# One VectorE pass fewer in turning float64 weights into float32

## The chip, the cores and the metric

The kernel runs on one core of a Trainium2 chip. The metric is the device time of one execution in microseconds, given as the median of a few runs; the less, the better.

## The reference

Three parts follow one another. First an attention over 16 heads (2 x 8) of 768 positions with 64 columns each, in which a query sees only keys of the same hash bucket; then two MLPs without bias, each 512 to 2048 to 512, over 1536 tokens.

```python
q_bits = (np.einsum('bhsd,dk->bhsk', q, proj) > 0)      # k_bits alike, six bits each
mask = q_bucket[:, :, :, None] == k_bucket[:, :, None, :]
scores = np.where(mask, scale * np.matmul(q, k.transpose(0, 1, 3, 2)), -1e9)
...
x = attn_out.transpose(0, 2, 1, 3).reshape(1536, 512)
h = x @ w_in;  x = (h / (1 + np.exp(-1.702 * h))) @ w_out       # first MLP
h = x @ w_in2; x = (h / (1 + np.exp(-h))) @ w_out2              # second MLP
```

`q`, `k`, `v` are float32, but the four weight matrices arrive as float64: they were scaled by a float64 number when drawn. No engine here works in float64, so the kernel takes each weight as two 32-bit words and builds the float32 value out of their bits.

## The kernel before, in words

**Weights.** Both MLPs cut their 2048 hidden columns into 16 blocks of 128. A block has two chunks, one of `w_in` and one of `w_out`, of 128 x 512 values each. There are 64 chunks in all. A chunk is loaded as int64 into `raw` (two buffers; L165 in the first MLP, L229 in the second), and `convert` (L113) makes float32 of it in `f`: ScalarE reads the upper word as if it were a float (L121), and four VectorE passes clamp it, shift its exponent, put the sign back and add the three lowest bits from the lower word (L122, L123, L124, L126). The value under work is `u`, one buffer in PSUM; for the first four chunks, which are converted before that buffer exists, it is `f` itself, in SBUF. Then `halves` (L130) splits `f` into a rounded half and the rest: ScalarE copies (L131), GpSimd subtracts (L132). The names `wih`, `wil`, `woh`, `wol` are these halves. In the first MLP 13 of the 16 blocks are also written to DRAM (L196, `spih` and so on) and read back later (L188).

**Attention.** Each of 96 steps takes 128 queries of a head: scores on TensorE (L520, L521) into `pss`, the row's minimum on VectorE (L528) into `p`, the exponential on ScalarE (L533), its f16 halves (L542 or L544, and L548 on GpSimd) in `hl`, a DMA that transposes two steps at once into `pt` (L554, on the queue of SP), and the product with `v` (L566 to L568) into `pav`. The result is turned and split into `XH` and `XL` (L594 to L601).

**Weaving.** After half of the heads the first batch is ready, and the first MLP works on it while attention goes on with the second batch: L742 is its first product, L721 to L726 its gate, L762 its second product, L771 the sum. Later the first MLP takes the second batch, and the second MLP (L807, L864, L874) ends the kernel. The second MLP forms some weights as sums of blocks (L283 to L286).

**What sets the order.** The code only says what depends on what. A planner places the instructions on the queue of each engine by priorities (the table `SOONER`, L80) and by its own simulated clock, and each engine then works its queue in order. A change in what one pass is thought to take can therefore move work on all engines.

Of the kernel before, what the change touches and what calls it, by code (L numbers as in the profile page):

```python
# [9 lines left out]
F32 = mybir.dt.float32  # L10
# [4 lines left out]
AF = mybir.ActivationFunctionType  # L15
ALU = mybir.AluOpType
# [5 lines left out]
def tile_lsh_attention_two_mlps(  # L22
# [13 lines left out]
    V, A, G, T, SP = nc.vector, nc.scalar, nc.gpsimd, nc.tensor, nc.sync  # L36
# [18 lines left out]
    VTOP = 2.0 ** 14  # L55
    MASK = 2.0 ** 30

    TINY = 2.0 ** -15
    HUGE = 122880.0 - 2.0 ** -7
    QSCALE = -1.0 / math.sqrt(D)  # L60
    assert math.frexp(QSCALE)[0] == -0.5
    NBUF = 3
# [50 lines left out]
    def convert(raw):  # L113
        word = raw.bitcast(I32).rearrange("p c (e w) -> p c e w", w=2)
        f = wpool.tile([P, NDC, P], F32, tag="f", name="f", bufs=FB)
        fi = f.bitcast(I32)

        u = work[0].tile([P, NDC, P], F32, tag="u", name="u") if work[0] is not None else f
        ui = u.bitcast(I32)
        top, bot = word[:, :, :, 1], word[:, :, :, 0]  # L120
        A.activation(u, top.bitcast(F32), AF.Abs)  # L121
        V.tensor_scalar(u, u, TINY, HUGE, op0=ALU.max, op1=ALU.min)  # L122
        V.tensor_scalar(ui, ui, 3, 0x3FFFFFFF, op0=ALU.logical_shift_left, op1=ALU.bitwise_and)  # L123
        V.scalar_tensor_tensor(out=ui, in0=top, scalar=-0x40000000, in1=ui,  # L124
                               op0=ALU.bitwise_and, op1=ALU.bitwise_or)
        V.scalar_tensor_tensor(out=fi, in0=bot, scalar=29, in1=ui,  # L126
                               op0=ALU.logical_shift_right, op1=ALU.bitwise_or)
        return f
# [5 lines left out]
    class Weights:  # L134
# [40 lines left out]
        def step(self):  # L175
            n = self.done
            while self.issued <= min(n + 1, len(self.chunks) - 1):
                self.fetch()
            i, kind = self.chunks[n]
            pool = self.pool_of(i)[0]  # L180
            hi = pool.tile([P, NDC, P], F32R, tag=f"w{kind}h", name=f"w{kind}h")
            lo = pool.tile([P, NDC, P], F32R, tag=f"w{kind}l", name=f"w{kind}l")
            block = self.order[i]
            self.t[i, kind] = hi, lo
            self.done += 1
            if self.again(n):
                for t, d in zip((hi, lo), self.kept.pop((block, kind))):
                    SP.dma_start(out=t.bitcast(F32), in_=d)  # L188
                return
            f = convert(self.raw.pop(n))  # L190
            halves(hi, lo, f)
            if self.last[block] > i:
                self.kept[block, kind] = []
                for t, part in ((hi, "h"), (lo, "l")):
                    d = spill.tile([P, NDC, P], F32, name=f"sp{kind}{part}{block[1]}")
                    SP.dma_start(out=d, in_=t.bitcast(F32))  # L196
                    self.kept[block, kind].append(d)
# [8 lines left out]
    class Pairs:  # L206
# [42 lines left out]
        def step(self):  # L249
# [4 lines left out]
            if how == "back":  # L254
                f = wpool.tile(whole, F32, tag="f", name="f", bufs=FB)
                SP.dma_start(out=f, in_=self.kept.pop(key))
            else:
                while len(self.raw) < 2 and self.sources:
                    self.fetch()
                f = convert(self.raw.pop(key))  # L260
# [846 lines left out]
```

## Time and profile before

| | |
|---|---|
| median of 3 runs | 789.61 us (784.69 to 790.25) |
| the profiled execution | 786.58 us |
| its span, first to last instruction | 784.8 us |
| mean granted TensorE clock | 0.972 of full speed |
| busy share PE / DVE / ACT / POOL | 92% / 71% / 56% / 62% |
| bytes moved by DMA | 124.82 MB, 159 GB/s over the span |

PE is TensorE, DVE VectorE, ACT ScalarE, POOL GpSimd; SP is the engine that only issues DMAs. A busy share is an average over a program with several regimes, so the rows below are cut by stretches: attention alone up to about 136 us, attention woven with the first MLP up to about 395 us, and the MLPs alone from there. A wait names the engine that was idle and the instruction that ended its idle time. The chain of waits follows the last instruction back to what released it, step by step; its shares say where the span went. DMA's share is the mean busy share of the 16 DMA engines and can pass 1, since packets overlap.

### The profile page before, as it was taken

What the parts mean: (1) busy time and instruction counts of PE and PEld (TensorE: products, weight loads), DVE (VectorE), ACT (ScalarE), POOL (GpSimd) and SP (SyncE); (2) the same over time, 40 slices, a digit from 0 to 9 for tenths busy, and PEclk for the clock granted to TensorE, in tenths of its full rate; (3) what the DMA queues carried; (4) which work ended last, traced back from release to release, by engine and by line L of the source; (5) the groups of instructions that cost most, each with busy time, mean ns of one, the idle gap of its engine ahead of it and who ended that gap; (6) DMA issues with size and microseconds to landing.
All of it is one profiled execution on the core that took longest, in us unless ns stands there. A gap on an engine that the chain in (4) does not pass through costs nothing.

```text
span 784.8 us, 14279 instructions
## 1 busy us (share of the span) xinstructions
PE 722.9 (92%) x5288; PEld 663.8 (85%) x5288; DVE 553.6 (71%) x1028; ACT 441.0 (56%) x767; POOL 488.1 (62%) x423
## 2 busy tenths in 40 slices
PE   6786777779899899899989999999999999999998
PEld 5676666668788899899989999999999998899886
DVE  8977688976789888797545777768334454687554
ACT  5866575777868677667556334445535333445330
POOL 5676576867667767567799624649627727457431
PEclk9898889799999999999999999999999999999999
DMA  5998999999998999797697675640001102021004
GB/s 161 188 202 192 185 195 211 214 248 225 270 254 244 255 255 265 192 222 174 106 320 255 230 257 175 212 136 0 28 1 55 55 0 54 28 81 53 1 2 160
DMA packets 200883, 124.82 MB, mean 159 GB/s; under 512 B 153831, under 2 KB 176359, under 8 KB 200813
## 3 DMA queue, kind: packets, MB, share of 16 engines
q1 hardware_dynamic: 200652, 123.91, 63.2%
q8 instruction: 41, 0.67, 0.3%
q14 instruction: 30, 0.24, 0.1%
q10 hardware_dynamic: 160, 0.00, 0.0%
HBM read 60.82 MB, written 20.97 MB: 104 GB/s over the span
## 4 chain that ended last, share of the span: by engine, by line
PE 65%; DMA 16%; DVE 7%; ACT 4%; issue 4%; POOL 3%; SPq 1%; DVEq 0%; POOLq 0%
PE psh L864 17%; PE psp L807 15%; DMA pt<-hl 11%; PE psp L762 6%; PE psp L742 6%; PE psh L742 5%; PE pso L762 5%; PE psh L762 3%; POOL hl L548 3%; DVE p L528 2%; PE pss L520 2%; ACT p L533 2%; DMA raw<-in_moe_w_out_dram 2%; PE pss L521 1%; PE pav L566 1%
## 5 line engine op out<-in xcount | busy, mean ns | idle before, releaser
L726 POOL TENSOR_TENSOR gl<-g,gh 128x384 fp32r<-128x384 f32 x128 | 129.2, 1017 | 130.2 <-ACT gh L725 117.3
L548 POOL TENSOR_TENSOR hl<-p,hl 128x768 f16<-128x768 f32 x96 | 162.7, 1702 | 71.3 <-ACT hl L544 34.6
L533 ACT ACTIVATE p<-p,lo 128x768 f32<-128x768 f32 x96 | 89.6, 937 | 51.8 <-DVE p L528 51.4
L874 DVE TENSOR_TENSOR part<-psh,part 128x512 f32<-128x512 f32 x84 | 58.1, 691 | 67.6 <-PE psh L864 67.3
L528 DVE TENSOR_SCALAR_CACHE_REDUCE p<-pss 128x768 f32<-128x768 f32 x96 | 90.8, 948 | 14.9 <-PE pss L521 13.2
L725 ACT CAST gh<-g 128x384 fp32r<-128x384 f32 x128 | 64.2, 512 | 52.5 <-PE psh L864 42.2
L566 PE MATMUL pav<-VS,pt 128*128 128x65 f16 x576 | 66.2, 200 | 29.4 <-DMA pt<-hl 27.5
L566 PEld LDWEIGHTS <-pt 128*128 128x128 f16 x576 | 55.6, 101 | 39.6 <-DMA pt<-hl 34.5
L520 PE MATMUL pss<-ak,aq 128*128 128x384 f32 x192 | 75.0, 392 | 10.3 <-DVE p L528 10.1
L724 ACT ACTIVATE g<-psp 128x384 f32<-128x384 f32 x88 | 43.2, 491 | 64.1 <-POOL gl L726 29.4
L864 PE MATMUL psh<-wol,gh 128*128 128x512 f32 x192 | 75.8, 395 | 0.0
L864 PE MATMUL psh<-woh,gl 128*128 128x512 f32 x192 | 75.6, 394 | 0.0
L864 PE MATMUL psh<-woh,gh 128*128 128x512 f32 x192 | 74.6, 389 | 0.0
L122 DVE TENSOR_SCALAR u<-u 128x512 f32<-128x512 f32 x60 | 41.7, 695 | 41.0 <-ACT u L121 40.9
L521 PE MATMUL pss<-BK,BQ 128*128 128x384 f32 x192 | 68.0, 355 | 0.0
L567 PE MATMUL pav<-VS,pt 128*128 128x64 f16 x576 | 66.3, 201 | 0.0
L568 PE MATMUL pav<-VS,pt 128*128 128x65 f16 x576 | 65.9, 199 | 0.0
L544 ACT CAST hl<-p 128x768 f16<-128x768 f32 x77 | 63.6, 829 | 2.1 <-DMA pt<-hl 1.1
L121 ACT ACTIVATE u<-raw 128x512 f32<-128x512 f32 x60 | 38.1, 634 | 45.1 <-DMA raw<-in_moe_w_out_dram 15.4
L132 POOL TENSOR_TENSOR wol<-f,woh 128x512 fp32r<-128x512 f32 x32 | 41.1, 1295 | 32.9 <-PE psh L864 20.4
L567 PEld LDWEIGHTS <-pt 128*128 128x128 f16 x576 | 56.4, 102 | 3.2 <-issue 3.2
L568 PEld LDWEIGHTS <-pt 128*128 128x128 f16 x576 | 56.5, 103 | 1.1 <-issue 1.1
(210 smaller groups left out, 2230.7 us busy)
## 6 DMA issues: line engine op xcount, KB each, us to landing
raw<-in_moe_w_in_dram SPq DMA_DIRECT2D x32, 512.0 KB
raw<-in_moe_w_out_dram SPq DMA_DIRECT2D x32, 512.0 KB
spih<-wih SPq DMA_DIRECT2D x13, 256.0 KB
spil<-wil SPq DMA_DIRECT2D x13, 256.0 KB
spoh<-woh SPq DMA_DIRECT2D x13, 256.0 KB
spol<-wol SPq DMA_DIRECT2D x13, 256.0 KB
wih<-spih SPq DMA_DIRECT2D x13, 256.0 KB
wil<-spil SPq DMA_DIRECT2D x13, 256.0 KB
```

The lines of the kernel that those rows point to most:

```text
L520: T.matmul(o, lhsT=lq, rhs=ak[:, half, :], start=True, stop=False)
L528: V.tensor_scalar(p, st.pop(("S", j)), LOW, None, op0=ALU.min, op1=ALU.min, accum_out=lo)
L533: A.activation(p, p, AF.Exp, bias=lo, scale=-1.0)
L548: G.tensor_tensor(out=hl[:, 1], in0=st.pop(("p", j))[0], in1=hl[:, 0], op=ALU.subtract)
L566: T.matmul(o, lhsT=pt[:, i], rhs=hv, start=(i == 0), stop=False)
L567: T.matmul(o[:, 0:D], lhsT=pt[:, i], rhs=lv, start=False, stop=False)
L568: T.matmul(o, lhsT=pt[:, NC + i], rhs=hv, start=False, stop=(i == NC - 1))
L726: G.tensor_tensor(out=gl, in0=g, in1=gh.bitcast(F32), op=ALU.subtract)
L742: T.matmul(h, lhsT=a[:, c], rhs=x[:, c, span(t)], start=(n == 0), stop=(n == 3 * NDC - 1))
L762: T.matmul(y, lhsT=w[:, o], rhs=g[:, f], start=(n == 0), stop=(n == 3 * nf - 1))
L807: T.matmul(o, lhsT=a, rhs=b, start=(n == 0), stop=(n == 5))
L864: T.matmul(y, lhsT=a[:, f, os_], rhs=x, start=(n == 0), stop=(n == 5))
```

## The change

ScalarE no longer takes the absolute value of the upper word but multiplies it by 2 to the power of -112, which lowers the exponent field in place. The clamp (L122) goes with its two constants. The next pass shifts left by three and masks nothing, since the shift itself drops the sign. The sign is then taken from the upper word by one bit in place of two.

```diff
--- before.py
+++ after.py
@@ -55,8 +55,7 @@
     VTOP = 2.0 ** 14
     MASK = 2.0 ** 30
 
-    TINY = 2.0 ** -15
-    HUGE = 122880.0 - 2.0 ** -7
+    DOWN = 2.0 ** -112
     QSCALE = -1.0 / math.sqrt(D)
     assert math.frexp(QSCALE)[0] == -0.5
     NBUF = 3
@@ -118,10 +117,9 @@
         u = work[0].tile([P, NDC, P], F32, tag="u", name="u") if work[0] is not None else f
         ui = u.bitcast(I32)
         top, bot = word[:, :, :, 1], word[:, :, :, 0]
-        A.activation(u, top.bitcast(F32), AF.Abs)
-        V.tensor_scalar(u, u, TINY, HUGE, op0=ALU.max, op1=ALU.min)
-        V.tensor_scalar(ui, ui, 3, 0x3FFFFFFF, op0=ALU.logical_shift_left, op1=ALU.bitwise_and)
-        V.scalar_tensor_tensor(out=ui, in0=top, scalar=-0x40000000, in1=ui,
+        A.activation(u, top.bitcast(F32), AF.Copy, scale=DOWN)
+        V.tensor_scalar(ui, ui, 3, None, op0=ALU.logical_shift_left)
+        V.scalar_tensor_tensor(out=ui, in0=top, scalar=-0x80000000, in1=ui,
                                op0=ALU.bitwise_and, op1=ALU.bitwise_or)
         V.scalar_tensor_tensor(out=fi, in0=bot, scalar=29, in1=ui,
                                op0=ALU.logical_shift_right, op1=ALU.bitwise_or)
```

Lines of the changed kernel stand two lower from the old L123 on and one lower before: the old L123 is L121, L124 is L122, L126 is L124, L165 is L163, L196 is L194, L520 is L518, L528 is L526, L554 is L552, L594 is L592 and L762 is L760.

The planner also places the work anew from the first conversion on. Three places show how.

VectorE, the first two conversions, which come before the first MLP's first product (`f` and `raw` as above; L528 makes `p`, L601 `XL`, L408 a rounded copy of `q` or `k`), before:

```order
L122 TENSOR_SCALAR f<-f 128x512
L528 TENSOR_SCALAR p,lo<-pss 128x768
L123 TENSOR_SCALAR f<-f 128x512
L601 TENSOR_TENSOR XL<-psx,XH 128x384
L408 CAST sq<-nq 128x6x64
L124 SCALAR_TENSOR_TENSOR f<-raw,f 128x512
L528 TENSOR_SCALAR p,lo<-pss 128x768
L601 TENSOR_TENSOR XL<-psx,XH 128x384
L122 TENSOR_SCALAR f<-f 128x512
L126 SCALAR_TENSOR_TENSOR f<-raw,f 128x512
L578 TENSOR_SCALAR ri<-pav,sv 128x3
L542 CAST hl<-p 128x768
```

and now:

```order
L121 TENSOR_SCALAR f<-f 128x512
L526 TENSOR_SCALAR p,lo<-pss 128x768
L122 SCALAR_TENSOR_TENSOR f<-raw,f 128x512
L599 TENSOR_TENSOR XL<-psx,XH 128x384
L406 CAST sq<-nq 128x6x64
L526 TENSOR_SCALAR p,lo<-pss 128x768
L124 SCALAR_TENSOR_TENSOR f<-raw,f 128x512
L599 TENSOR_TENSOR XL<-psx,XH 128x384
L121 TENSOR_SCALAR f<-f 128x512
L540 CAST hl<-p 128x768
```

The four passes of a conversion are three, and the passes between them are the same ones in nearly the same order; the second conversion begins one row after the first has ended, where it began one row before.

SP, the DMAs around the 24th and 25th transpose (`raw` a load of weights, `sp..` halves written to DRAM, L432 and L384 loads for attention), before:

```order
L165 DMA raw<-in_moe_w_out_dram 128x512
L196 DMA spih_2208<-wih 128x512
L554 DMA_TRANSPOSE pt<-hl 128x24x128
L196 DMA spil_2210<-wil 128x512
L165 DMA raw<-in_moe_w_in_dram 128x4x128
L554 DMA_TRANSPOSE pt<-hl 128x24x128
L196 DMA spoh_2315<-woh 128x512
L196 DMA spol_2317<-wol 128x512
L165 DMA raw<-in_moe_w_out_dram 128x512
L554 DMA_TRANSPOSE pt<-hl 128x24x128
```

and now:

```order
L163 DMA raw<-in_moe_w_out_dram 128x512
L194 DMA spih_2205<-wih 128x512
L552 DMA_TRANSPOSE pt<-hl 128x24x128
L194 DMA spil_2207<-wil 128x512
L163 DMA raw<-in_moe_w_in_dram 128x4x128
L194 DMA spoh_2311<-woh 128x512
L163 DMA raw<-in_moe_w_out_dram 128x512
L552 DMA_TRANSPOSE pt<-hl 128x24x128
L194 DMA spol_2313<-wol 128x512
L552 DMA_TRANSPOSE pt<-hl 128x24x128
```

A load of `raw` that stood behind the second transpose in these rows stands ahead of it.

TensorE, where the first MLP's second product begins (`pso` its sums; `pss` scores, `psx` the turn of a finished block, `pstr` of a new head, `pav` the product with `v`), before:

```order
L416 MATMUL pstr<-identr,sq 128x128 x3
L520 MATMUL pss<-ak,aq 128x384
L521 MATMUL pss<-BK_153,BQ_149 128x384
L520 MATMUL pss<-ak,aq 128x384
L521 MATMUL pss<-BK_153,BQ_149 128x384
L594 MATMUL psx<-ident,xn 128x128 x3
L762 MATMUL pso<-gh,woh 128x384 x2
L416 MATMUL pstr<-identr,sq 128x128 x3
L566 LDWEIGHTS pt
```

and now:

```order
L519 MATMUL pss<-BK_152,BQ_148 128x384
L760 MATMUL pso<-gh,woh 128x384 x2
L518 MATMUL pss<-ak,aq 128x384
L519 MATMUL pss<-BK_152,BQ_148 128x384
L518 MATMUL pss<-ak,aq 128x384
L519 MATMUL pss<-BK_152,BQ_148 128x384
L760 MATMUL pso<-gl,woh 128x384
L760 MATMUL pso<-gh,wol 128x384
L760 MATMUL pso<-gh,woh 128x384
L760 MATMUL pso<-gl,woh 128x384
L760 MATMUL pso<-gh,wol 128x384
L760 MATMUL pso<-gh,woh 128x384
```

Before, two products of L762 stood ahead of the weight load of `pt` that ends the first piece and begins the `pav` of a pair. Now 18 of them stand ahead of that same weight load, 16 more.

## Rows read from the trace of the kernel before

**Rows 1.** Page, part 1: busy us, share of the span, instructions of each engine.

```profile
PE 722.9 (92%) x5288; PEld 663.8 (85%) x5288; DVE 553.6 (71%) x1028; ACT 441.0 (56%) x767; POOL 488.1 (62%) x423
```

**Rows 2.** Windows view, five stretches: length, busy us (instructions) of each engine, clock, DMA.

```profile
core 0: us, PE busy (x) PEld busy (x) DVE busy (x) ACT busy (x) POOL busy (x), PEclk, DMA share, GB/s
0.00:136.00 136.00, 101.56 (x1068) 85.65 (x1069) 110.65 (x236) 91.09 (x134) 89.10 (x68) 0.89 0.92 189
136.00:172.00 36.00, 25.87 (x298) 22.51 (x296) 31.01 (x57) 23.91 (x37) 24.89 (x16) 0.86 1.07 234
172.00:280.00 108.00, 99.34 (x896) 90.49 (x897) 85.00 (x165) 81.48 (x138) 78.42 (x62) 0.98 1.07 251
280.00:395.00 115.00, 112.45 (x1014) 107.00 (x1014) 90.79 (x185) 79.44 (x130) 79.94 (x62) 1.00 0.84 195
395.00:785.00 390.00, 383.69 (x2019) 358.14 (x2017) 236.10 (x389) 165.04 (x333) 215.77 (x217) 1.00 0.32 105
```

**Rows 3.** Chain of waits in 395 to 785 us, shares by line.

```profile
by line: PE psh L864 34.0%; PE psp L807 30.0%; PE psp L762 12.1%; PE psp L742 11.7%; PE psh L762 5.1%; PE psh L742 4.3%; DMA wih<-spih 1.0%; ACT L724 0.3%; DVE part L874 0.2%; ACT u L121 0.2%; ACT gh L725 0.1%; ACT g L724 0.1%; SPq L188 0.1
```

**Rows 4.** Waits of PE, 136 to 172, then 172 to 280: us, times, longest.

```profile
PE pav L566 <- DMA pt<-hl: 3.2, 2, 2.7
PE pss L520 <- DVE p L528: 3.1, 4, 1.8
PE psh L742 <- DVE XL L601: 1.6, 1, 1.6
...
PE pav L566 <- DMA pt<-hl: 5.7, 5, 1.5
```

**Rows 5.** Groups by line and form: count, busy us, mean ns, idle before.

```profile
L122 DVE TENSOR_SCALAR u<-u 128x512 f32<-128x512 f32 x60 | 41.7, 695 | 41.0 <-ACT u L121 40.9
L122 DVE TENSOR_SCALAR f<-f 128x512 f32<-128x512 f32 x4 | 2.7, 671 | 2.4 <-ACT f L121 2.4
L123 DVE TENSOR_SCALAR u<-u 128x512 int32<-128x512 int32 x60 | 41.7, 694 | 0.9
L121 ACT ACTIVATE u<-raw 128x512 f32<-128x512 f32 x60 | 38.1, 634 | 45.1 <-DMA raw<-in_moe_w_out_dram 15.4 <-DMA raw<-in_moe_w_in_dram 14.6 <-DVE f L126 13.9
L423 ACT ACTIVATE aq<-pstr 128x384 fp32r<-128x384 f32 x32 | 15.4, 488 | 6.0 <-PE pstr L416 5.8
L528 DVE TENSOR_SCALAR_CACHE_REDUCE p<-pss 128x768 f32<-128x768 f32 x96 | 90.8, 948 | 14.9 <-PE pss L521 13.2 <-POOL hl L548 1.5
```

**Rows 6.** Source view: L121 on `f`; L122 in 172:280, 280:395, 395:785 (min/median/max ns).

```profile
L121 ACT ACTIVATE f<-raw x4: 661/674/719, 137.0 to 164.8; 128x512 f32<-128x512 f32 x4
...
L122 DVE TENSOR_SCALAR u<-u x15: 677/695/700, 181.6 to 276.3; 128x512 f32<-128x512 f32 x15
...
L122 DVE TENSOR_SCALAR u<-u x13: 680/696/700, 283.9 to 361.7; 128x512 f32<-128x512 f32 x13
...
L122 DVE TENSOR_SCALAR u<-u x32: 689/699/700, 395.1 to 724.3; 128x512 f32<-128x512 f32 x32
```

**Rows 7.** Chain of waits in order of time: L122 in 136 to 280 (start, us).

```profile
165.46 0.04 DVE f L122
...
190.49 0.70 DVE u L122
...
221.38 0.71 DVE u L122
...
240.32 0.61 DVE u L122
...
246.98 0.68 DVE u L122
```

**Rows 8.** Chain of waits by line, 172 to 280, then 280 to 395.

```profile
by line: DMA pt<-hl 26.1%; issue 8.9%; DMA nv<-in_v_dram 6.9%; POOL hl L548 5.9%; DMA raw<-in_moe_w_in_dram 5.1%; DVE p L528 4.9%; PE pso L762 4.5%; DMA raw<-in_moe_w_out_dram 3.5%; ACT p L533 2.9%; DVE u L122 2.5%; PE pav L566 2.3%; POOL g
...
by line: PE pso L762 27.5%; PE psh L742 20.2%; DMA pt<-hl 17.3%; PE pss L520 5.0%; PE pss L521 4.6%; PE pav L566 3.7%; PE pav L567 3.3%; PE pav L568 3.2%; DMA raw<-in_moe_w_out_dram 3.1%; PE psbit L448 2.4%; SPq L188 1.4%; POOL hl L548 1.4%
```

**Rows 9.** Page, part 6, size of a load; chain of waits, 24 products back to back.

```profile
raw<-in_moe_w_in_dram SPq DMA_DIRECT2D x32, 512.0 KB
...
285.86 4.16 PE psh L742 x24
```

**Rows 10.** Tile view of `pt`, 172 to 395 us: transposes, and what PE waits for.

```profile
L554 SPq DMA_TRANSPOSE pt<-hl x24: 3596/4400/7652, 167.5 to 383.3; - x24
...
its engine sat idle before it (us, times) until:
  DMA pt<-hl: 20.1, 20
```

## The prediction

> **What bounds the kernel now.** I read the page's busy shares first, then the same engines stretch by stretch, then the chain of waits in each stretch, and last the waits of TensorE. Over the whole span TensorE (PE) is busy for 92% and VectorE (DVE) for 71% [rows 1]. That average hides three regimes [rows 2]. From 0 to 136 us, attention alone, nothing that the change touches runs: the first conversion starts at 137. From 395 us to the end PE is busy 383.7 of 390 us at full clock, so at most 6.3 us could be had there, and the chain of waits of that stretch is PE almost throughout [rows 3]. Between lies the stretch where attention is woven with the first MLP and where 32 of the 64 conversions run. There PE is idle 10.1 us from 136 to 172, 8.7 us from 172 to 280 and 2.6 us from 280 to 395: 21.4 us in all. That is the ceiling of what the change can give, since the work of PE itself is the same.
>
> In 136 to 172 VectorE is the fullest of the five engines, 31.0 of 36 us; in 172 to 280 it is busy 85.0 of 108, PE 99.3, and the DMA engines have a share of 1.07; in 280 to 395 PE has 112.5 of 115 [rows 2]. What PE waits for tells the same: from 136 to 172 it waits 3.1 us for `p` of L528 and 1.6 us for `XL` of L601, both VectorE's, and 3.2 us for the transposes `pt`; from 172 to 280 the largest wait, 5.7 us, is for `pt` [rows 4].
>
> **What the change removes.** One VectorE pass for each conversion, L122. Of 64 passes 60 work on `u` in PSUM at 695 ns, four on `f` in SBUF at 671 ns [rows 5]: 41.7 + 2.7 = 44.4 us of VectorE busy time. What this is worth depends on where they lie [rows 6].
>
> From 136 to 172: four passes, 2.7 us of the 31.0. VectorE works its queue in order, so a pass of L528 behind an L122 starts earlier by that pass, and PE waits 4.7 us here for VectorE [rows 4]. On the chain the pass itself is only 0.04 us [rows 7]; but it stands between ScalarE's pass and a long L123. I take 2 us, between 0 and the whole 2.7.
>
> From 172 to 280: 15 passes, 10.4 us. The chain of waits passes through L122 with 2.5% of 108 us, four pieces of 0.70, 0.71, 0.61 and 0.68 us, together 2.7 us [rows 7, 8]. I take these 2.7 us as the gain. The low end is 0 (the transposes, 26.1% of that chain, are then late in their place); the high end is PE's whole idle time, 8.7 us.
>
> From 280 to 395: 13 passes, 9.0 us, none with a share of the chain, which is PE's products and transposes [rows 8]. What hides them is PE, which is idle only 2.6 us. Gain 0, at most 2.6. If that cover were gone (PE waiting instead of working), each pass could cost up to its 0.7 us.
>
> From 395 on: 32 passes of 0.70 us, 22.4 us, hidden below the same full PE. I cost them at 0. VectorE will only wait longer for PE's products, as it does now.
>
> **What it alters.** ScalarE's `Abs` (634 ns for 512 columns) becomes a scaled copy. The nearest scaled copy, L423, takes 488 ns for 384 columns [rows 5]. In proportion to the columns that is 651 ns, and not less than the 488 of the narrower one; 64 times the difference to 634 is between +1.1 and -9.3 us of ScalarE, which is busy 56% [rows 1]. I take no change. L123 loses its mask but stays one pass over the same tile; L122 and L123, a float and an integer pass of two operations, differ by 1 ns [rows 5], so I keep 694 ns. L528, a pass over 768 columns of PSUM in 948 ns [rows 5], would by its columns give 632 ns, 3.7 us less of VectorE busy time over 60 passes, none of it counted. The mask constant of L124 costs nothing: the same pass.
>
> **What it moves.** The planner places everything from the first conversions on anew. On SP the queue holds one load of `raw` more ahead of a transpose from the sixth transpose after the conversions start; the shift stays at about one. A load is 512 KB [rows 9], at 251 GB/s [rows 2] 2.1 us of all DMA engines. It also brings weights to PE sooner. On PE 16 products of L762 now stand ahead of the first `av` of a pair that stood ahead of them before: 16 times 0.173 us (24 products in 4.16 us, [rows 9]) is 2.8 us of work taken forward, which fills idle time if `woh` and `wol` are there and holds up attention if they are not. I cost the moves at 0 and keep 3 us either way for the range.
>
> Sum: 2 + 2.7 + 0 + 0 = 4.7 us. The profiled execution took 786.58 us (span 784.8 and 1.8 around it), so 781.9. It lies 3.0 us under the median of the runs, 789.61 (784.69 to 790.25); counted from that median the sum gives 784.9. I forecast the middle, **783.5 us**; the forecast's own range is 779 to 788.
>
> The Trainium skill, Perfetto Trace Analysis, section Identifying the Most-Contended Engine, says to optimise the engine with the highest occupancy first, which speaks against this change: VectorE is second at best. By that rule taken over the whole span the sum would be 0 in place of 4.7 us; taken by stretch, the trace supports it from 280 us on and not from 136 to 172, where VectorE is the fullest.
>
> **The rivals.** (a) *The cover holds*: no gain. PE waits for transposes and weights that come through full DMA engines (share 1.07 from 136 to 280, [rows 2]), and VectorE's hop in the chain is replaced by another that ends as late. For it: L122 waits 40.9 us for ScalarE over the run [rows 5], so part of the removed time becomes waiting for the same ScalarE result, now in front of L123. Against it: PE's waits for VectorE from 136 to 172. Time: 786.6 to 789.6. The same section of the Trainium skill warns that the occupancy of 16 DMA engines misleads and wants the memory's rate instead; the rate here is 251 GB/s from 172 to 280, and no run before the change shows how much more there is.
>
> (b) *VectorE paces the woven stretch*: its queue delays each step of attention, and every pass removed from 136 to 280 comes back whole: 2.7 + 10.4 = 13.1 us of the 18.8 that PE idles there. For it: 85.0 of 108 us busy in a queue that works in order. Against it: PE's longest wait there is for `pt`. Time: 773.5 from the profile, 776.5 from the median; say 775.
>
> (c) *Slower: the loads run into the transposes.* The place is SP's queue and the DMA engines from 172 on. A faster VectorE frees `raw` sooner, and loads and spills that now stand ahead land in front of transposes that PE already waits for 20.1 us in 20 places [rows 10]. There are 24 transposes from 172 to 395 [rows 10]; if each lands 0.46 us later, a fifth of one load's 2.1 us, PE waits 11 us more and the gain is gone: 797.6 from the profile, 800.6 from the median. It decides from there; below 0.2 us each, 4.7 us in all, the gain and the loss cancel. For it: PE has `av` ahead of MLP products in its order, so it cannot step around a late transpose. Against it: weights that come sooner feed PE as well.
>
> (d) *The change doesn't do what it says*: the scaled copy from the strided word costs far more than `Abs`, and ScalarE, not VectorE, becomes late. From the rows, at most 1.1 us.
>
> **How the numbers follow.** Three runs of the kernel spread over 0.7%, so 1% (7.9 us) is about what a measurement can tell from no change: faster means under 781.7, slower over 797.5. Forecast 0.45, (a) 0.25, (b) 0.15, (c) 0.13, (d) 0.02. A third of the forecast's 0.45 lies under 781.7, so faster is 0.15 + 0.15 = 0.30; slower is (c), 0.13; the rest, 0.57, is within 1%. The range runs from 774, which takes in most of (b), to 796, which takes in (a), (d) and the 3 us of the moves on top, and leaves out most of (c) and the edge of (b).
>
> **What the profile after would show.** Right: 64 passes fewer on VectorE and its busy time near 509 us (553.6 less 44.4); PE's idle time from 136 to 280 down by 4 to 5 us, PE's waits for `p` and `XL` shorter; from 395 us or so on no change but an earlier start; ScalarE's pass at 620 to 650 ns and L123 at 690 ns. Wrong, for (a): VectorE's 44 us turned into waiting for ScalarE and DMA with PE's gaps as before. For (b): the second MLP starts 10 us earlier or more. For (c): PE's waits for `pt` from 172 on well over 20 us. What would break the sum most easily is the new order of PE and SP, whose cost I took as 0 without a row that shows it.

## The result, and the profile after

The changed kernel takes 792.83 us (median of 15 runs, 790.81 to 796.15) where the kernel before takes 786.65 us in the same comparison (15 runs, 782.80 to 790.85): a ratio of 1.0063, 95% interval 1.0045 to 1.0080. (The two medians alone would make 1.0079; the argument goes by the ratio, since it comes with an interval.) It is slower by 0.6%, some 5 to 6 us; the forecast was 783.5 us, 3.1 less than the profiled execution of before. The profiled execution of the change took 791.26 us, its span 789.5.

The page after, busy time of each engine, answers to [rows 1]:

```profile
PE 725.7 (92%) x5288; PEld 668.1 (85%) x5288; DVE 512.3 (65%) x964; ACT 438.2 (56%) x767; POOL 487.4 (62%) x423
```

VectorE has 64 instructions less, as the change says, and 41.3 us less of busy time, where the forecast had 44.4; no other engine's work has moved by more than 4.3 us. The conversion's passes, by line and form (count, busy us, mean ns, idle before; L121 is the old L123, L120 the old L121), answer to [rows 5]:

```profile
L121 DVE TENSOR_SCALAR u<-u 128x512 int32<-128x512 int32 x60 | 41.8, 696 | 59.6 <-ACT u L120 59.5
L120 ACT ACTIVATE u<-raw 128x512 f32<-128x512 f32 x60 | 38.1, 635 | 62.9 <-DMA raw<-in_moe_w_in_dram 36.6 <-DMA raw<-in_moe_w_out_dram 22.4 <-DVE f L124 3.6
```

Each pass costs what it did: 696 ns for 694, 635 for 634. But VectorE now waits 59.5 us for ScalarE's pass (40.9 in [rows 5]), and ScalarE waits 59.0 us for loads of `raw` (30.0 there). The windows view, columns as in [rows 2]:

```profile
136.00:172.00 36.00, 28.85 (x305) 25.46 (x305) 29.20 (x54) 23.98 (x38) 25.88 (x18) 0.79 1.04 240
172.00:280.00 108.00, 98.05 (x876) 90.14 (x874) 77.41 (x150) 81.05 (x138) 78.23 (x61) 0.98 1.04 256
280.00:395.00 115.00, 110.07 (x972) 104.41 (x973) 78.47 (x162) 75.76 (x122) 75.73 (x59) 0.99 0.80 183
395.00:785.00 390.00, 388.37 (x2078) 362.83 (x2076) 218.47 (x364) 166.37 (x337) 220.02 (x221) 1.00 0.32 106
```

TensorE (PE) idles 17.1 us from 136 to 280, 1.7 less than before, but its granted clock from 136 to 172 is 0.79 of full speed, where it was 0.86 [rows 2]. From 280 to 395 it idles 4.9 us, where it was 2.6, and there its clock is 0.99, no longer 1.00. From 395 on it is busy 388.4 us of 390, where it was 383.7. The first product of the second MLP (source view, first and last start), before and then after:

```profile
L807 PE MATMUL psp<-XH,wih x128: 333/334/346, 526.9 to 754.3; 128*128 128x384 f32 x128
```

```profile
L805 PE MATMUL psp<-XH,wih x128: 333/334/340, 531.6 to 760.4; 128*128 128x384 f32 x128
```

It starts 4.7 us later, which is the whole difference of the spans (789.5 and 784.8). So the loss lies ahead of 526.9 us.

To find it I took, for the first product with `v` of each of the 96 steps (counted from 0), its start less the work that stands ahead of it in PE's queue, priced at full clock from the rows (0.174 us for a product of 384 columns): this is the time PE has lost up to there, in waits and in clock. It is worked out from one execution of each kernel. Up to step 81 (337.3 us before, 335.3 after) the two kernels have lost 100.2 and 101.0 us. Up to step 84 (351.5 and 359.8) it is 101.1 and 106.2: **5.2 us go in these three steps, where 0.9 went before**. Behind them the difference stays at 4.7 to 5.7 us. (Executions scatter: e3 and e4 below have the change's order up to step 78, and had lost 1.5 and 1.7 us more there than the change.) The timeline of the change at that place (start, length, engine, line; in brackets the idle time before and what ended it):

```profile
333.29 0.57 SPq L163 DMA_DIRECT2D raw<-in_moe_w_in_dram  x1
...
335.29 0.94 DVE L526 TENSOR_SCALAR_CACHE_REDUCE p<-pss 128x768 f32<-128x768 f32 x1
...
337.56 0.64 ACT L120 ACTIVATE u<-raw 128x512 f32<-128x512 f32 x1 [2.71 <-DMA raw<-in_moe_w_in_dram]
338.13 0.92 ACT L531 ACTIVATE p<-p,lo 128x768 f32<-128x768 f32 x1
...
339.08 0.83 ACT L542 CAST hl<-p 128x768 f16<-128x768 f32 x1
...
339.99 1.67 POOL L546 TENSOR_TENSOR hl<-p,hl 128x768 f16<-128x768 f32 x1 [2.79 <-ACT hl L542]
...
341.69 4.18 SPq L552 DMA_TRANSPOSE pt<-hl  x1
...
348.76 0.23 PE L564 MATMUL pav<-VS,pt 128*128 128x65 f16 x1 [2.43 <-DMA pt<-hl]
```

VectorE has `p` ready at 336.2. ScalarE's next row is a conversion pass, which waits for its load until 337.56; the exponential (L531) of the ready `p` stands behind it in the queue and starts at 338.13. That is 1.9 us after `p` was ready, and each link behind it follows the one before by no more than 0.1 us: rounding, GpSimd's half, the transpose. PE, which needs the transpose, stands 2.43 us. Then its granted clock falls (5 us slices, columns as above):

```profile
345.00:350.00 5.00, 2.57 (x32) 2.26 (x31) 2.93 (x6) 2.41 (x4) 3.47 (x3) 0.88 1.23 240
350.00:355.00 5.00, 5.00 (x38) 5.00 (x36) 3.20 (x8) 2.83 (x5) 2.64 (x2) 0.78 0.87 223
```

12% and 22% of 5 us make 1.7 us of work lost, in a stretch that had full clock before (1.00 from 280 to 395 us, [rows 2]).

**Theory 1**: the planner's new order costs, not the passes, and above all this row. **Rival 2**: the new passes cost wherever they stand. **Rival 3**: shorter passes free `raw` sooner, and the loads run into the transposes.

### The profile page after: what moved, and what is told of

Its sections match the earlier page's. It is cut to its first block, busy times and chain, and to the rows that moved or that the text cites. A ratio compares the mean times of both kernels' runs of the same rounds, so it can differ in the third digit from the quotient of the medians.

```text
span 789.5 us, 14224 instructions
## 1 busy us (share of the span) xinstructions
PE 725.7 (92%) x5288; PEld 668.1 (85%) x5288; DVE 512.3 (65%) x964; ACT 438.2 (56%) x767; POOL 487.4 (62%) x423
## 4 chain that ended last, share of the span: by engine, by line
PE 65%; DMA 16%; DVE 7%; ACT 5%; issue 3%; POOL 3%; SPq 0%; DVEq 0%; POOLq 0%; ACTq 0%
PE psh L862 17%; PE psp L805 15%; DMA pt<-hl 12%; PE psp L760 6%; PE psp L740 6%; PE psh L740 5%; PE pso L760 4%; DMA raw<-in_moe_w_in_dram 3%; PE psh L760 3%; DVE p L526 2%; PE pss L518 2%; PE psbit L446 2%; ACT p L531 2%; PE pav L564 1%; PE pss L519 1%
## 5 line engine op out<-in xcount | busy, mean ns | idle before, releaser
L531 ACT ACTIVATE p<-p,lo 128x768 f32<-128x768 f32 x96 | 89.6, 936 | 48.9 <-DVE p L526 48.4
L526 DVE TENSOR_SCALAR_CACHE_REDUCE p<-pss 128x768 f32<-128x768 f32 x96 | 90.7, 948 | 15.5 <-PE pss L519 8.3
L564 PEld LDWEIGHTS <-pt 128*128 128x128 f16 x576 | 55.8, 101 | 43.8 <-DMA pt<-hl 40.1
L518 PE MATMUL pss<-ak,aq 128*128 128x384 f32 x192 | 76.3, 398 | 9.7 <-DVE p L526 9.3
L121 DVE TENSOR_SCALAR u<-u 128x512 int32<-128x512 int32 x60 | 41.8, 696 | 59.6 <-ACT u L120 59.5
L120 ACT ACTIVATE u<-raw 128x512 f32<-128x512 f32 x60 | 38.1, 635 | 62.9 <-DMA raw<-in_moe_w_in_dram 36.6
L519 PE MATMUL pss<-BK,BQ 128*128 128x384 f32 x192 | 69.8, 364 | 0.1
L566 PE MATMUL pav<-VS,pt 128*128 128x65 f16 x576 | 65.8, 200 | 0.0
L740 PE MATMUL psh<-XH,wih 128*128 128x384 f32 x160 | 55.5, 347 | 3.8 <-ACT wih L129 2.9
L565 PEld LDWEIGHTS <-pt 128*128 128x128 f16 x576 | 56.6, 102 | 2.4 <-issue 2.3
L130 POOL TENSOR_TENSOR wol<-f,woh 128x512 fp32r<-128x512 f32 x32 | 41.3, 1306 | 27.2 <-PE psh L862 25.2
```

Of the source, the lines that this page charges most:

```text
L518: T.matmul(o, lhsT=lq, rhs=ak[:, half, :], start=True, stop=False)
L519: T.matmul(o, lhsT=bq, rhs=bk[:, half * HS:(half + 1) * HS], start=False, stop=True)
L526: V.tensor_scalar(p, st.pop(("S", j)), LOW, None, op0=ALU.min, op1=ALU.min, accum_out=lo)
L531: A.activation(p, p, AF.Exp, bias=lo, scale=-1.0)
L564: T.matmul(o, lhsT=pt[:, i], rhs=hv, start=(i == 0), stop=False)
L565: T.matmul(o[:, 0:D], lhsT=pt[:, i], rhs=lv, start=False, stop=False)
```

## The experiments

B is the kernel before in the same runs (786.7 to 788.4 us), and a ratio is to it; "B + 3.1" compares medians. Most experiments hold every queue to a written order: at the end of the kernel each instruction is chained behind the one that is to precede it on its engine, without a wait. No run holds the change to its own whole order, so what the chains cost by themselves is not measured. They neither slow e1, which is as fast as the kernel before without them, nor cure e2 and e13, which lose time with them; and in the pairs e13 and e14, e1 and e9 both kernels have them.

```diff
+    ORDER = {'Activation': (...), 'DVE': (...), ...}   # ranks in the order of the code
+    ...
+        for a, b in zip(row, row[1:]):
+            tc.add_manual_dep(traced[engine][b], traced[engine][a].name, behind, reason="order")
```

| run | passes | order | us | ratio, 95% |
|---|---|---|---|---|
| the change | 3 | its own | 792.83 | 1.0063 (1.0045 to 1.0080) |
| e1 | 3 | of before | 785.75 | 0.9988 (0.9964 to 1.0011) |
| e2 | 4 | of the change | 801.27 | 1.0180 (1.0156 to 1.0204) |
| e3 | 3 | of the change, one row moved | 789.86 | 1.0039 (1.0014 to 1.0064) |
| e4 | 3 | of the change, from 331 us of before | 788.52 | 1.0021 (1.0004 to 1.0038) |
| e5 | 2 | of before | 785.33 | 0.9973 (0.9953 to 0.9993) |
| e6 | 3 | drawn anew, weights sooner | 791.73 | 1.0058 (1.0035 to 1.0081) |
| e7 | 3 | of the change, nine rows moved | 791.96 | 1.0051 (1.0030 to 1.0071) |
| e8 | 3 | of before, nine rows moved | 787.73 | 1.0000 (0.9985 to 1.0015) |
| e9 | 3 | of before, the row put ahead | 787.18 | 0.9985 (0.9964 to 1.0005) |
| e10 | 4 | drawn anew, weights sooner | 800.27 | 1.0147 (1.0112 to 1.0181) |
| e11 | 4 | drawn anew, other rate | 790.17 | 1.0023 (0.9996 to 1.0050) |
| e12 | 3 | drawn anew, other rate | 793.14 | 1.0070 (1.0043 to 1.0097) |
| e13 | 3 | of before, from 331 us of the change | 794.90 | 1.0069 (1.0046 to 1.0093) |
| e14 | 3 | as e13, one row moved | 790.10 | 1.0023 (1.0003 to 1.0043) |

### Passes against order: e1 and e2

The edit of e1 is the one above on the changed kernel, with the ranks of the kernel before; that of e2 the same on the kernel before, with the ranks of the change.

> The change's three passes, with every engine's queue held to the order of the kernel before (its L122 rows taken out). Written against the kernel before in the same runs, called B (786.7 in the last ones; the change stood at B + 6.2). Theory 1, the new order is what costs, not the passes: B - 5 to B, as the shorter passes can only bring things forward. Rival 2, the new passes themselves cost, wherever they stand: B + 4 to B + 7. Rival 3, shorter passes free raw sooner, and the loads then run into the transposes whatever the order: B + 2 to B + 5.

> The four passes of the kernel before, with every engine's queue held to the order of the changed kernel, L122 put right ahead of each L123. Theory 1 (the order costs): B + 5 to B + 10, the change's loss and the longer conversions on top. Rival 2 (the passes cost): B - 1 to B + 1. Rival 3 (sooner loads): B to B + 2, since VectorE frees raw as late as before.

e1 is as fast as the kernel before, e2 slower than the change. Rival 2 wanted +4 to +7 and -1 to +1, rival 3 +2 to +5 and 0 to +2: both are out, and the order costs 0.75% (1.0063 less 0.9988), **5.9 us**, by the two intervals something between 3.6 and 8.2. In the two traces e1 ends 4.0 us ahead of the change (spans 785.5 and 789.5), and 3.8 of that is lost between steps 81 and 84: 1.4 us in e1, 5.2 in the change. e2 came out at +14.5, over the +10 that I gave it. By the same reckoning it has no single place: against the kernel before it loses 4.1 us up to step 81, 3.6 from there to step 84 and 3.4 behind the last step. What does it was not followed up.

But e1 gives no gain of 5 us either. The waits of PE from 136 to 280 us in e1 (engine, line, what for: us, times, longest):

```profile
PE pav L564 <- DMA pt<-hl: 16.3, 12, 3.5
PE pss L518 <- DVE p L526: 2.9, 3, 2.1
...
PE psh L740 <- DVE XL L599: 1.5, 1, 1.5
```

The waits of scores and first products for VectorE, 4.7 us in [rows 4] and 0.8 more from 172 to 280, are down to 4.4; the wait for transposes has grown from 8.9 us [rows 4] to 16.3. In all PE idles 20.6 us there in e1, where it was 18.8, and its granted clock is 0.96, where it was 0.95. The earlier start is spent at the next gate. What a pass is worth depends on the order itself: the fourth costs 0.12% in the old one (e1, not clear of zero by its interval) and 1.17% in the change's (e2 against the change).

### A second pass less: e5

```diff
         V.tensor_scalar(ui, ui, 3, None, op0=ALU.logical_shift_left)
-        V.scalar_tensor_tensor(out=ui, in0=top, scalar=-0x80000000, in1=ui,
-                               op0=ALU.bitwise_and, op1=ALU.bitwise_or)
```

> As the three passes in the old order, with the sign pass (the changed kernel's L122) left out as well, so that a conversion is two VectorE passes; its weights have lost their signs. Written against the kernel before, B (three passes in the old order stood at B - 1.0). If VectorE's passes lie on the path of the woven stretch, as the forecast took it (4.7 us for one pass fewer): B - 6. If other waits cover them (rival (a) of the prediction): B - 2 to B, no more than a microsecond from three passes, with TensorE's waits for pt as long or longer.

-1.9 us: the covered case. Windows view of e5 from 136 to 280 us, and its waits of PE there:

```profile
136.00:280.00 144.00, 125.35 (x1216) 115.08 (x1215) 93.68 (x182) 106.17 (x175) 102.02 (x78) 0.96 1.03 248
```

```profile
PE pav L562 <- DMA pt<-hl: 15.0, 10, 3.0
...
PE pss L516 <- DVE p L524: 0.8, 2, 0.5
```

VectorE is busy 93.7 us here, where the kernel before had 31.0 and 85.0, together 116.0 [rows 2]; PE waits 0.8 us for `p`, and still 15.0 for `pt`. In the old order two VectorE passes fewer in each conversion are worth 1.9 us by the medians, between 0.6 and 3.7 by the interval; one is worth 1.0, which can't be told from zero.

### The row at 337 us: e3, e7, e8, e9

The edit of e3, in ScalarE's queue:

```diff
 L723 CAST gh<-g 128x384
-L120 ACTIVATE u<-raw 128x512
-L531 ACTIVATE p<-p,lo 128x768
-L542 CAST hl<-p 128x768
+L531 ACTIVATE p<-p,lo 128x768
+L542 CAST hl<-p 128x768
+L120 ACTIVATE u<-raw 128x512
```

> The changed kernel with one row of ScalarE's queue moved: the conversion pass that waited 2.71 us for its load at 334.9 to 337.6 us stands behind the exponential and the rounding that were right behind it, not ahead of them. Theory 1 in its narrow form (this one pass blocks the queue, the transpose behind it comes late and TensorE's clock falls): 2 to 5 us less than the change, so B + 1 to B + 4. Theory 1 in its wide form (many places add up), rival 2 and rival 3: no difference to the change, B + 6.

+3.1 us, in the range of the narrow form, but its interval touches the change's, so the time alone doesn't settle it. The timeline of e3:

```profile
336.87 0.95 DVE L526 TENSOR_SCALAR_CACHE_REDUCE p<-pss 128x768 f32<-128x768 f32 x1
...
341.47 3.58 SPq L552 DMA_TRANSPOSE pt<-hl  x1
...
341.49 0.44 PE L760 MATMUL pso<-gh,woh 128*128 128x384 f32 x1 [1.07 <-DVE part L769]
...
348.89 0.20 PE L564 MATMUL pav<-VS,pt 128*128 128x65 f16 x1 [0.51 <-DMA pt<-hl]
```

From the row minimum to the transpose it takes 4.60 us, 1.80 less than the 6.40 of the change; PE's wait for it at 348.89 is 0.51 us, the clock stays at 1.00 to 365 us, and PE loses 2.3 us between steps 81 and 84 in place of 5.2. VectorE, behind the later conversion, costs PE 0.5 us more at L760 (1.07 us for 0.59 in the change). By the clock of the trace the transpose is only 0.2 us earlier than in the change, since this execution came to the place 1.6 us later; what counts is the way from the row minimum to it.

e7 does the same at nine places of the change's order, e8 at nine places of the old order (each a conversion pass right ahead of an exponential):

> The changed kernel with nine rows of ScalarE's queue moved: every conversion pass of the woven stretch that stands right ahead of an exponential which does not depend on it stands behind that exponential, and behind its rounding where that follows. One of the nine is the row moved alone, which stood at B + 3.1 against B + 6 of the change. If conversion passes that wait for their loads ahead of exponentials are what the new order costs (theory 1 in its wide form): B - 1 to B + 2. If only that one place counts: B + 3. If moving them makes VectorE late instead, since its queue waits for their results: B + 4 to B + 8.

> The three passes in the old order with the same edit there (nine conversion passes of ScalarE put behind the exponential right behind them). If waiting for loads ahead of exponentials costs in the old order too: B - 4 to B - 2, better than both kernels. If the old order had them where they cost nothing: as three passes in the old order, B - 2 to B.

Neither gains: e7 stands at +4.7, e8 at +0.5. In e7 the loss between steps 81 and 84 is 2.4 us as in e3, but PE has lost 5 us more by step 81 than in the change (106.0 for 101.0), and still 3.4 us more than in e3. ScalarE's wait from 172 to 280 us in e7, and then in the change:

```profile
ACT p L531 <- DVE p L526: 12.5, 11, 3.1
```

```profile
ACT p L531 <- DVE p L526: 6.3, 7, 3.1
```

VectorE's queue now stands waiting for the conversions that were put back (17.5 us for ScalarE's pass in this stretch, 11.8 in the change), with `p` behind them. So it isn't that a conversion pass ahead of an exponential costs as such. e9 tests that from the other side, with the row put ahead in the old order:

```diff
 L723 CAST gh<-g 128x384
+L120 ACTIVATE u<-raw 128x512
 L531 ACTIVATE p<-p,lo 128x768
 L542 CAST hl<-p 128x768
-L120 ACTIVATE u<-raw 128x512
```

> The reverse of the one row moved, in the order that had no loss: three passes in the old order, and there the same chunk's conversion pass on ScalarE put ahead of the exponential and the rounding that stood before it, so that they wait for its load. If a conversion pass that blocks exponentials behind it makes the transpose late and TensorE wait (theory 1's mechanism): 2 to 4 us more than three passes in the old order (B - 1.0), so B + 1 to B + 3, and in the trace the conversion pass waits 2 to 5 us with the exponential ready, the transpose after next starts later by 1 to 3 us, and TensorE's idle time grows by 2 to 4 us between 337 and 370 us. If ScalarE's waits are covered: B - 2 to B, with no more idle time there.

My theory missed: -0.7 us, no loss. The wait is there in the timeline of e9, longer than in the change, and so is the late transpose (345.32 in e1):

```profile
341.21 0.64 ACT L120 ACTIVATE u<-raw 128x512 f32<-128x512 f32 x1 [4.79 <-DMA raw<-in_moe_w_in_dram]
...
347.26 4.58 SPq L552 DMA_TRANSPOSE pt<-hl  x1
...
353.64 0.20 PE L564 MATMUL pav<-VS,pt 128*128 128x65 f16 x1 [1.58 <-DMA pt<-hl]
```

PE stands 1.58 us, its clock stays at 1.00, and it loses 2.3 us between steps 81 and 84, 0.9 more than in e1. In the old order the exponential that is held back is the first of its pair: it starts at 341.78, 5.5 us ahead of the transpose, where the change has 3.6 us. That this is why it costs less there is not tested: the transpose came 1.9 us later than in e1 all the same, and what differs from the change is PE's shorter wait and the clock that did not fall.

### Which half of the order, and how much is that row: e4, e13, e14

e4 takes the change's order up to about 331 us and the old one from there; e13 the reverse; e14 is e13 with the edit of e3.

> The three passes; every queue in the change's order up to about 331 us (just ahead of the place at which TensorE lost 5 us), and from there in the order of the kernel before. Theory 1 in its narrow form: the loss is gone, B to B + 1.5, as TensorE stood 0.8 us behind at that point. Theory 1 in its wide form: B + 2 to B + 4. Rivals 2 and 3: B + 4 to B + 7.

> The reverse of the new order that turns old: three passes, every queue in the order of the kernel before up to the same point (about 331 us), and from there in the change's order. If the change loses its time behind that point: B + 3 to B + 5 (three passes in the old order B - 1, and 4 to 5 us on top), with TensorE's idle time growing by 4 to 5 us between 335 and 362 us. If it loses it ahead of that point, or all over: B - 1 to B + 2.

> As the old order that turns new, with the one row of ScalarE's queue moved behind its exponential and rounding. If that row is more than half of what is lost behind the turn: 2 to 3.5 us less than without the move, and idle time of TensorE between 335 and 362 us of 2 to 2.5 us in place of 4 to 5. If the row is an incident and the rest of the order carries the loss: no difference of more than 1 us.

e4 loses 1.7 us, between what the narrow form (0 to 1.5) and the wide one (2 to 4) gave it, e13 6.5, over the 5 I gave it, and e14 1.7. The pair e13 and e14 differs by one row of ScalarE's queue and by 0.46%, 3.6 us, and the intervals don't meet: **the row is a cause**. The timeline of e13 and then of e14:

```profile
339.41 0.95 DVE L526 TENSOR_SCALAR_CACHE_REDUCE p<-pss 128x768 f32<-128x768 f32 x1
...
341.76 0.63 ACT L120 ACTIVATE u<-raw 128x512 f32<-128x512 f32 x1 [2.79 <-DMA raw<-in_moe_w_in_dram]
...
345.88 4.79 SPq L552 DMA_TRANSPOSE pt<-hl  x1
...
352.90 0.20 PE L564 MATMUL pav<-VS,pt 128*128 128x65 f16 x1 [2.36 <-DMA pt<-hl]
```

```profile
340.62 0.95 DVE L526 TENSOR_SCALAR_CACHE_REDUCE p<-pss 128x768 f32<-128x768 f32 x1
...
343.38 0.62 ACT L120 ACTIVATE u<-raw 128x512 f32<-128x512 f32 x1
...
345.22 3.59 SPq L552 DMA_TRANSPOSE pt<-hl  x1
...
352.60 0.20 PE L564 MATMUL pav<-VS,pt 128*128 128x65 f16 x1 [0.46 <-DMA pt<-hl]
```

It repeats the change and e3: 6.47 us from minimum to transpose against 4.60, a wait of PE of 2.36 against 0.46, and between steps 81 and 84 a loss of 5.3 against 2.4 us. The clock in e13, and then in e14:

```profile
350.00:355.00 5.00, 2.64 (x41) 2.32 (x40) 2.31 (x6) 1.72 (x5) 2.69 (x3) 0.83 0.94 273
355.00:360.00 5.00, 5.00 (x26) 5.00 (x25) 3.95 (x10) 3.53 (x6) 2.64 (x2) 0.83 0.89 180
```

```profile
350.00:355.00 5.00, 4.54 (x56) 4.22 (x55) 4.48 (x10) 3.91 (x7) 3.79 (x3) 1.00 0.69 210
355.00:360.00 5.00, 5.00 (x33) 4.96 (x32) 4.95 (x12) 4.20 (x8) 4.04 (x4) 1.00 0.87 167
```

So the row costs 1.9 us of PE's wait, less 0.5 that VectorE takes back, and 1.7 us of clock: 3.1 us by the traces, one execution of each. e13 and e14 both lose another 4 us between steps 78 and 81, at the turn from one order to the other; so e13 alone doesn't size the second half of the change's order.

### Other plans: e6, e10, e11, e12

```diff
-    SOONER = (..., {'scores': 200, ...
+    SOONER = (..., {'weights': 30, 'scores': 200, ...
```

is the edit of e6 (on the change) and e10 (on the kernel before);

```diff
-    RATE = (3.4, 2.85)
+    RATE = (3.6, 2.85)
```

that of e11 (before) and e12 (the change). All four do the same work in an order drawn anew.

> The changed kernel with one entry more in the planner's table ('weights': 30 in the woven stage), which makes it place everything anew from the conversions on; the work is the same. If any new plan scatters by some microseconds around what the plan before gave, whatever it moves: anywhere from B - 3 to B + 9, with gaps of TensorE in other places than the change has them. If the change's plan is unlucky at one place only: B to B + 2. If putting conversions sooner makes ScalarE's queue wait for loads (theory 1's mechanism): B + 6 or more, with ScalarE's waits for raw longer than the 59 us of the change.

> The kernel before, with its four passes, and the entry 'weights': 30 in the planner's table as in the run of the change with that entry (B + 4.5): another plan for the same work as before. If the plan of the kernel before is one that happened to come out well and another plan loses, whatever the passes: B + 2 to B + 8. If plans for four passes are as good as one another and the change's plans alone are bad: B - 2 to B + 1.

> The kernel before with 3.6 in place of 3.4 units of the first MLP woven into a step of attention (until three quarters of the heads), another plan for the same work. If other plans of the four passes lose: B + 2 to B + 8. If they don't: B - 2 to B + 1.

> The changed kernel with the same 3.6 in place of 3.4: a third plan for the three passes. If plans scatter by some microseconds whatever the passes: anywhere from B - 3 to B + 9, as likely under the change's B + 5 as over it. If three passes were worth the forecast's gain in a plan drawn for them: B - 5 to B - 2. If only plans for three passes are bad: B + 4 to B + 8.

Every other plan is slower than the one of the kernel before: with four passes +14.5 (e2), +12.4 (e10, over the +8 I gave it) and +2.3 us (e11, whose interval reaches no change), with three +6.2, +4.5 and +5.3 (the change, e6, e12). e6 has its loss elsewhere: 1.3 us between steps 81 and 84. Plans scatter by more than ten microseconds over equal work, and the kernel before has the best of those seen; no run here beats it by more than the measurement tells, save e5, which leaves out the sign pass. e1 keeps the three passes and is 0.75% under the change.

## Why the prediction was wrong

**The step that failed** is "I cost the moves at 0 and keep 3 us either way for the range". Moved rows cost 5.9 us in place of 0 (e1 against the change), twice the bound, and more than the whole gain of 4.7. I had looked at the places where loads went ahead of transposes and products ahead of `av`; the row that costs lay on ScalarE, where the prediction compared no rows. Of the 5.9 us about 3 are that one row: 3.1 by the traces (PE's wait and the clock), 3.6 by the ratios of e13 and e14, 1.9 by those of the change and e3, whose intervals overlap. The rest has no sure place: the traces of e1 and the change put all but 0.2 us of their difference between steps 81 and 84, but by the times e4, which has none of the second half, still stands 0.33%, 2.6 us, over e1, and its turn may have a part in that. This rest is not traced to rows, and stays open. Nor is it shown why the planner put the row there; that it takes loads to land sooner than they do is a guess.

**TensorE's clock** has no term in the sum. The prediction calls PE's idle time, 21.4 us, the ceiling, though [rows 2] show a clock of 0.86 from 136 to 172 us and 0.98 from 172 to 280. Of the 3.1 us of the row 1.7 are clock, and the change's clock from 136 to 172 fell to 0.79.

**The gain** of 2 + 2.7 us from 136 to 280 was the wrong size: 1.0 us of 4.7 in the order held (e1, between -0.9 and 2.8 by its interval). VectorE's pieces on the chain [rows 7, 8] and PE's waits for `p` and `XL` [rows 4] were real, and they shrank; the wait for `pt` took them over. That is rival (a), which had a chance of 0.25 and which e5 shows at a second pass: 8.9 us of waits for `pt` before, 16.3 and 15.0 with one and two passes fewer. The sum of the chain's pieces was no estimate of the gain here, but at best an upper bound.

**280 to 395 at 0**: right for the passes (PE is busy 111.91 of 115 us in e1, 112.45 in [rows 2]) and wrong for the order, which lost its time here. The text named the condition, a cover that goes when PE waits, and gave it no chance.

**From 395 on at 0**: right, to the microsecond; the lead or lag at 395 us is carried to the end.

**ScalarE's pass and L123 at no change**: right (635 and 696 ns); rival (d) is out. **Rival (b)**, VectorE as the pace: out, by e5. **Rival (c)** had the sign and the gate but the wrong mechanism. It took the 20.1 us of [rows 10] for PE's wait, but that line adds up the waits of products and of weight loads, which overlap; PE idles only 11.2 us in this stretch [rows 2]. The same tile view also says who waited for the transposes (us, times). Here are its lines for the products of L566, before and then after:

```profile
  PE pav L566: 8.1, 8
```

```profile
  PE pav L564: 10.0, 9
```

In e1, which loses nothing, it is 11.9 us, so this sign doesn't tell a slower kernel from one that isn't. The transposes did not get slower where the time was lost: from the start of the record on SP's queue to PE's product it takes 7.1 us in the change and 7.0 in e13, 7.4 in e3 and e14. Nor did the transposes' records on SP's queue get longer over the stretch, as the tile view of the change shows, with 4234 ns in the middle where [rows 10] has 4400:

```profile
L552 SPq DMA_TRANSPOSE pt<-hl x24: 3572/4234/6590, 169.5 to 392.4; - x24
```

The one that cost was issued late. And e1, which frees `raw` as soon as three passes can in the old order, loses nothing.

The Trainium skill, Perfetto Trace Analysis, section Identifying the Most-Contended Engine, puts the engine with the highest occupancy first. The runs agree for this kernel: VectorE, second at best over the span, gave back 1.0 us (between -0.9 and 2.8) for 36.6 us of busy time taken off it in e1, and 1.9 us for 78.2 in e5.

## What to carry to other kernels

Where a planner or a priority list sets the order, an edit that only shortens work is two edits; hold the old order and make the edit alone before you believe either sign, and don't count on the next order drawn: of those seen here the old one was the best. A queue worked in order turns a load that lands late into a delay for whatever stands behind its consumer: look on every engine for a pass that waits for a DMA with ready work right behind it, and try the move at that place alone, since nine such moves gained nothing (e7, e8) and one put in at another place cost nothing clear (e9). Time taken out of one gate counts only up to the next one, so sum the waits of the bound engine over all gates, not the one that shrinks.

## What the runs showed of the hardware

I had not expected a wait of 2.4 us to be followed by another 1.7 us lost in clock. In the two traces in which PE stood 2.43 and 2.36 us for this transpose (the change, e13), the granted clock of the following slices was 0.88 and 0.78, and 0.83 and 0.83, 3.4 us of the time at the lower of its two levels, 1.2 in place of 2.4 GHz; each time 1.7 us of work was lost. In the three in which it stood 0.51, 0.46 and 1.58 us (e3, e14, e9) the clock of those slices stayed at 1.00. The length of the wait alone doesn't decide it, as other waits for `pt` in the same traces show: in e14 1.87 us of wait up to 272.3 us were followed by 3.4 us at the lower level, while after 2.56 us of wait up to 281.8 us in e3, and 2.08 us up to 322.7 us in the kernel before, the clock stayed at 1.00. So the 1.7 us belong to the executions that were traced; how often a late transpose here costs them is not measured. The load at that place also took 4.3 us from its issue (333.29) to ScalarE's start, where its 512 KB at the 195 GB/s of that stretch before [rows 2, 9] would be 2.7 us.
